# Channel attention and two feed-forward layers in one kernel: operands of the second pair prepared beside the last plain units, Silu ahead of a split, the last q and k tiles loaded singly

## The chip, the core and the metric

The kernel runs on one core of a Trainium2 chip. The metric is device time in microseconds of one execution; the median of three runs is given. Engines are named as in the profile: PE or TensorE (matmul), PEld (its weight loads), DVE (VectorE), ACT (ScalarE), POOL (GpSimd), SP (SyncE, which issues the DMAs).

## What is computed

Three steps over N = 6016 tokens and C = 256 channels, in float32:

```python
qn = q / (norm(q, axis=1) + 1e-6); kn = k / (norm(k, axis=1) + 1e-6)   # norms over the tokens
a  = softmax(kn.T @ qn / tau)                                          # 256 x 256
x  = v @ a                                                             # 6016 x 256
x  = (silu(x @ w_gate) * (x @ w_val)) @ w_out                          # layer 1: 256 -> 1536 -> 256
h  = x @ w_in;  x = (h * clip(h + 3, 0, 6) / 6) @ w_out2               # layer 2: 256 -> 2048 -> 256
```

The weights reach the core as 64-bit floats.

## The kernel before

**Accuracy.** Each matmul of the feed-forward layers is made of three (mm3, L91): every operand is split into a high part (ACT copies it to a rounded type) and a low part (DVE subtracts the high part from the original), and high x high, low x high and high x low are summed. So every operand of a matmul costs one ACT and one DVE instruction, each of 128x512 as a rule.

**Weights.** Each tile of 64-bit weights is a Job (L103): load, cut (two DVE instructions: exponent and mantissa bits), power (two ACT activations), mantissa and sign (DVE), scale (DVE product), and for w_out a split into `wo`. pump (L271) moves three jobs one step each; the jobs of layer 1 run during the plain units. convert (L252) moves the jobs of layer 2, whose scalings, sums and subtractions are on POOL, and stores the result in memory (wi_d, w2_d).

**Attention.** q and k are read in chunks of 1, 1, 2, then fourteen of 3, then one of 1 tile of 128 tokens, five chunks ahead (L410 to L420); ACT squares them, DVE adds the squares up in acc, TensorE accumulates k.T q. norms (L487) sums acc over the tokens and makes the two scalings; softmax follows. TensorE transposes the result into `early`. keep_warm (L434) issues matmuls whose result is not used.

**Folding.** v @ a is never formed: a is multiplied into w_gate and w_val instead. fold(m, g) (L606) multiplies one weight tile on TensorE, ACT scales the result out of the bank into FA, then ACT and DVE split it into the layer's weights w1. The closures that it returns (`lows`) are the DVE splits; those of the first two folds are called once by hand and again in unit 1, since the list is not emptied between.

**Plain units.** The tokens are six pairs of two blocks (512 tokens each, the last pair 448). Pair 0 is computed plainly: 24 units (L904), one for each of 12 tiles of the hidden layer and each of two blocks: twelve matmuls into two banks, ACT takes Silu of one, DVE multiplies by the other, the product h is split into hl, and three units later back() (L824) multiplies it by `wo` (six matmuls, tile `o`). ps_f has four banks (a, d, b0, b1), taken in turn.

**Cubes.** The other pairs go through seven products instead of eight (class Cube, L673; p1 to p7, three matmuls each) for a 2x2 arrangement of two hidden tiles and two blocks. Their seven operands, sums and differences of the four quarters of x, are made by prep(u) (L327): nine steps s1 to s9, each a split or a difference, put in the list `todo`; work(n) (L396) runs n steps of that list. Each split operand lies in a staging tile (stage, L320: two tiles `st`, or operand tiles that are free), is stored to memory, and is loaded again when its pair begins (arrive, L951; load_op, L400). In a cube ACT copies p1's bank (a) into bank b, applies Silu to bank a after p2 (after_p2, L774) and to x12 after p3 (after_p3, L780). The split of cube i's r11 stands in late3 (L812), which the loop (L962) calls in cube i+1 ahead of that cube's p2. layer 2's cubes have a clipped product in place of Silu.

**What sets the order.** The program is scheduled by hand (L407): each engine runs its instructions in the order in which the code issues them, and waits on semaphores for the other engines. prep(1) is appended to `todo` behind the last weight sums, by a step that issues its load (prep_steps, L388); it starts in unit 22, and the rest is run by arrive(1, ...) behind the last unit.

Of the kernel before, what the change touches and what calls it, by code (L numbers as in the profile page):

```python
# [18 lines left out]
def channel_attention_then_two_ffns(  # L19
# [24 lines left out]
    nc = tc.nc  # L44
# [273 lines left out]
    places_st = [0]  # L318

    def stage(u):  # L320

        i = places_st[0] = places_st[0] + 1
        if 0 < u < NP or u >= NP and i % 4 < 2:
            return op_p.tile([P, 2, TB], F32R, tag=f"op{(NQ * (u + 1) + i % 2) % NS}", name="sp")
        return st_p.tile([P, 2, TB], F32R, tag="st", name="st")

    def prep(u):  # L327

        n = pairs[u % NP][1]
        x = load_v(u) if u < NP else load_x2(u - NP)  # L330
        b11, b21, b12, b22 = x[:, 0, 0, :n], x[:, 0, 1, :n], x[:, 1, 0, :n], x[:, 1, 1, :n]
        opd[u] = dram.tile([P, NQ, 2, TB], F32, tag=f"opd{u}", name="opd")
        of = {0: b11, 1: b11, 2: b22, 3: b21, 4: b22, 5: b12, 6: b21}
        t = {}

        def hi(j):
            t[j] = stage(u - 1)
            nc.scalar.activation(t[j][:, 0, :n], of[j], AF.Copy)

        def lo(j):  # L340
            nc.vector.tensor_tensor(  # L341
                out=t[j][:, 1, :n], in0=of[j], in1=t[j][:, 0, :n].bitcast(F32), op=ALU.subtract
            )
            stored.add((u, j))
            nc.sync.dma_start(out=opd[u][:, j, :, :n], in_=t[j][:, :, :n].bitcast(F32))

        def diff(out, a, b):
            nc.vector.tensor_tensor(out=out, in0=a, in1=b, op=ALU.subtract)  # L348

        def s1():  # L350
            hi(0)

        def s2():
            hi(4)
            lo(0)
# [32 lines left out]
    def prep_steps(u):  # L388
        def load():
            todo[2:2] = prep(u)  # L390

        return [load, lambda: None, lambda: None]

# [13 lines left out]
    with tc.manual_schedule():  # L407

        with tc.tile_pool(name="sm", bufs=1) as sm, tc.tile_pool(name="qk", bufs=AHEAD) as qk_p, tc.tile_pool(
# [5 lines left out]
            while sum(sizes) < NT:  # L415
                sizes.append((NT - sum(sizes) + 1) // 2)
# [13 lines left out]
            WARM = (1, 11, 2)  # L430
# [56 lines left out]
            def norms():  # L487
# [11 lines left out]
                v_hi(0)  # L499
# [3 lines left out]
                )  # L503
                nc.scalar.activation(nrm, ss_ps, AF.Sqrt, bias=tiny)
# [23 lines left out]
            for i, (n0, n) in enumerate(chunks):  # L528
# [10 lines left out]
                if i == len(chunks) - 2:  # L539
                    nc.vector.tensor_tensor(out=acc[:, 1], in0=acc[:, 1], in1=acc[:, 2], op=ALU.add)  # L540
                if i == len(chunks) - 1:
                    nc.vector.tensor_tensor(out=acc[:, 0], in0=acc[:, 0], in1=acc[:, 1], op=ALU.add)
# [18 lines left out]
            pump(steps=(1,))  # L561
# [16 lines left out]
            pump(steps=(2,))  # L578
# [9 lines left out]

            keep_warm(WARM[2])
# [16 lines left out]
        def fold(m, g):  # L606
# [15 lines left out]
            fa = FA[g % 2]  # L622
            for c in range(CT):
                nc.scalar.activation(fa[:, (c, 3 - c)[m]], ps[:, c, :], AF.Copy, scale=rden[:, c : c + 1])
            o = CT * m
# [47 lines left out]
        class Cube:  # L673
# [106 lines left out]
            def after_p3(self):  # L780
                self.add(self.x12, self.x12, self.d)
                if self.layer == 1:
                    self.silu(self.x12)
                else:
                    hl = self.hi(self.r11)
                    self.lo(hl, self.r11, 0, 0)
                    self.r12 = self.relu(self.x12)
# [24 lines left out]
            def late3(self):  # L812
                x = self.r11 if self.layer == 1 else self.r21
                self.lo(self.hi(x), x, 0, 1)
# [62 lines left out]
        pump(steps=(2,))  # L877
        nc.scalar.activation(warm, three, AF.Silu)
        need(0, 0)
        need(1, 0)  # L880
        lows = [fold(0, 0)]
        v_hi(1)
        lows.append(fold(1, 0))
        pump(steps=(3, 2))
        for go in lows:
            go()
        v_lo(1)
        pump(steps=(1,))
        todo.append(w1_sums(0))

# [13 lines left out]
        for i, (f, b) in enumerate(units):  # L904
# [27 lines left out]
            work(2 if i > 18 else 1)  # L932
            g = i // 4 + 1
            if i % 4 in (1, 2) and g < NG1:
# [13 lines left out]
        plain_split(lambda: pump())  # L948
        todo[:0] = w1_rest(NG1 - 1)

        def arrive(u, n, *js):  # L951
            for j in js:
                while (u, j) not in stored:
                    work(1)
                load_op(u, j, n)

        arrive(1, pairs[1][1], 0, 1)
        arrive(1, pairs[1][1], 2, 3, 4, 5, 6)
# [3 lines left out]
        for c, key in enumerate(cubes):  # L962
# [15 lines left out]
            if layer == 1 and c % 4 == 1 and not converted():  # L978
                convert()
# [21 lines left out]
            cube.after_p3()  # L1001
# [52 lines left out]
```

## Time and profile before

| | |
|---|---|
| median of three runs | 1142.75 us (1142.6 to 1143.39) |
| the profiled execution | 1143.76 us, span 1142.0 us |
| TensorE busy | 1106.2 us (97%), 4900 matmuls |
| DVE, ACT, POOL busy | 807.2 (71%), 760.2 (67%), 81.4 us (7%) |
| mean granted TensorE clock | 0.989 |
| DMA | 157.65 MB, mean 138 GB/s |

The span runs from the first to the last instruction of the program; the profiled execution's own time has 1.76 us more. A matmul's end is modelled, so "busy" of TensorE says little about its pace; what it waits for, and the clock that it was granted, say more. Roughly: attention to 57 us, the plain units of pair 0 to 178 us, layer 1's cubes to 640 us, layer 2's cubes to the end.

### The profile page before, as it was taken

The page shows a single profiled execution, that of the slowest core. Times are in us where ns is not written, and L with a number is a line of the kernel's source. Part 1 is how long each engine was busy: PE and PEld are TensorE (multiplying, and loading weights), DVE is VectorE, ACT ScalarE, POOL GpSimd, SP SyncE. Part 2 cuts the span into 40 slices and gives each one's busy share as a digit, 9 for nine tenths or more (in the row PEclk, how much of TensorE's full clock was granted, in tenths as well). Part 3 has the DMA queues.
Part 4 walks back from the last instruction along what each step waited for, and adds up shares of the span by engine and source line. Part 5 has one row for each costly group of instructions (what it writes and reads, how often), then busy time and mean ns, then how long its engine had stood idle before and what let it go on. Part 6 is the DMA issues. An engine that isn't in the chain of part 4 may idle for free.

```text
span 1142.0 us, 13730 instructions
## 1 busy us (share of the span) xinstructions
PE 1106.2 (97%) x4900; PEld 918.4 (80%) x4900; DVE 807.2 (71%) x1252; ACT 760.2 (67%) x1323; POOL 81.4 (7%) x92
## 2 busy tenths in 40 slices
PE   8989995999999999999999999999999999999998
PEld 6768883877877877788899888888888888888897
DVE  6989953577787777766566568667677677676665
ACT  6767643566766766675566577677767777776766
POOL 0000000122322222320000000000000000000000
PEclk9999997999999999999999999999999999999999
DMA  8622305433733634532355752422523413414100
GB/s 327 253 74 93 129 1 195 173 132 118 247 135 130 230 143 148 200 134 84 115 187 203 273 192 93 148 111 82 177 88 113 168 56 130 142 65 131 68 1 32
DMA packets 58340, 157.65 MB, mean 138 GB/s; under 512 B 5280, under 2 KB 17312, under 8 KB 56864
## 3 DMA queue, kind: packets, MB, share of 16 engines
q1 hardware_dynamic: 58272, 156.78, 38.4%
q8 instruction: 38, 0.62, 0.2%
q14 instruction: 30, 0.25, 0.1%
HBM read 93.45 MB, written 63.31 MB: 137 GB/s over the span
## 4 chain that ended last, share of the span: by engine, by line
PE 67%; DVE 14%; ACT 7%; DMA 3%; issue 3%; DVEq 0%; SPq 0%; ACTq 0%
PE o L96 31%; PE ps_b L96 15%; PE ps_d L96 10%; PE ps_a L96 10%; ACT hl L702 3%; DVE h L759 3%; DVE hl L768 2%; DVE h L706 2%; DMA op<-opd 1%; DVE sp L341 1%; ACT e L127 1%; ACT e L126 1%; DMA vr<-in_vT 1%; DVE vr L348 1%; ACT h L702 1%
## 5 line engine op out<-in xcount | busy, mean ns | idle before, releaser
L768 DVE TENSOR_TENSOR hl<-h,hl 128x512 fp32r<-128x512 f32 (+1 forms) x312 | 211.9, 692 | 210.2 <-ACT hl L702 205.0
L96 PE MATMUL o<-hl,w2o 128*128 128x512 f32 (+1 forms) x1152 | 287.6, 385 | 0.0
L702 ACT ACTIVATE hl<-h 128x512 fp32r<-128x512 f32 (+1 forms) x312 | 188.0, 618 | 100.0 <-DVE h L752 53.5
L96 PEld LDWEIGHTS o<-hl,w2o 128*128 128x128 f32 x1152 | 216.0, 188 | 40.8 <-DVE hl L768 0.7
L96 PE MATMUL o<-hl,wo 128*128 128x512 f32 (+1 forms) x864 | 220.3, 391 | 0.0
L96 PEld LDWEIGHTS o<-hl,wo 128*128 128x128 f32 x864 | 164.0, 190 | 31.4
L96 PE MATMUL ps_b<-op,w 128*128 128x512 f32 (+1 forms) x540 | 142.0, 388 | 3.1 <-DMA op<-opd 3.1
L96 PEld LDWEIGHTS ps_b<-op,w 128*128 128x128 f32 x540 | 101.1, 188 | 24.9 <-issue 3.8
L96 PE MATMUL ps_a<-op,w 128*128 128x512 f32 (+1 forms) x360 | 102.2, 392 | 14.4 <-DMA op<-opd 9.9
L96 PE MATMUL ps_b<-op,w2i 128*128 128x512 f32 (+1 forms) x432 | 112.0, 385 | 0.0
L96 PE MATMUL ps_d<-op,w 128*128 128x512 f32 (+1 forms) x360 | 102.9, 394 | 2.6 <-DVE h L706 1.7
L96 PEld LDWEIGHTS ps_b<-op,w2i 128*128 128x128 f32 x432 | 81.1, 188 | 15.1
L702 ACT ACTIVATE h<-ps_b 128x512 f32<-128x512 f32 (+1 forms) x108 | 63.3, 586 | 43.5 <-PE ps_b L96 41.9
L96 PEld LDWEIGHTS ps_a<-op,w 128*128 128x128 f32 x360 | 67.0, 190 | 31.1 <-ACT h L741 8.3
L746 ACT ACTIVATE h<-h,three 128x512 f32<-128x512 f32 (+1 forms) x96 | 68.7, 716 | 33.3 <-DVE h L706 31.7
L706 DVE TENSOR_TENSOR h<-h,ps_b 128x512 f32<-128x512 f32 (+1 forms) x108 | 72.4, 671 | 15.6 <-PE ps_b L96 15.3
L96 PEld LDWEIGHTS ps_d<-op,w 128*128 128x128 f32 x360 | 66.9, 190 | 19.9 <-DVE h L706 6.6
L96 PE MATMUL ps_d<-op,w2i 128*128 128x512 f32 (+1 forms) x288 | 79.8, 385 | 0.3 <-DMA op<-opd 0.3
L96 PE MATMUL ps_a<-op,w2i 128*128 128x512 f32 (+1 forms) x288 | 79.8, 385 | 0.0
L706 DVE TENSOR_TENSOR h<-h,ps_d 128x512 f32<-128x512 f32 (+1 forms) x108 | 72.2, 669 | 10.3 <-PE ps_d L96 10.3
L702 ACT ACTIVATE ps_b<-ps_a 128x512 f32<-128x512 f32 (+1 forms) x108 | 61.9, 573 | 25.9 <-PE ps_a L96 25.7
L752 DVE SCALAR_TENSOR_TENSOR h<-h 128x512 f32<-128x512 f32 (+1 forms) x96 | 65.1, 678 | 12.6 <-ACT h L746 12.6
(128 smaller groups left out, 1321.2 us busy)
## 6 DMA issues: line engine op xcount, KB each, us to landing
op<-opd SPq DMA_DIRECT2D x63, 512.0 KB, 5.0
opd<-sp SPq DMA_DIRECT2D x42, 512.0 KB, 2.7
opd<-st SPq DMA_DIRECT2D x21, 512.0 KB, 2.6
raw<-in_moe_w_out SPq DMA_DIRECT2D x14, 512.0 KB, 4.2
w2i<-wi_d SPq DMA_DIRECT2D x4, 1792.0 KB, 8.2
op<-opd SPq DMA_DIRECT2D x14, 448.0 KB, 4.2
tq<-in_q SPq DMA_DIRECT2D x14, 384.0 KB, 6.7
tk<-in_k SPq DMA_DIRECT2D x14, 384.0 KB, 7.2
```

Of the source, the lines that this page charges most:

```text
L96: nc.tensor.matmul(out, lhsT=w, rhs=x, start=first, stop=last, skip_group_check=True)
L126: nc.scalar.activation(e.bitcast(F32), e, AF.Relu, scale=-4.0, bias=exp_top)
L127: nc.scalar.activation(e, e.bitcast(F32), AF.Relu, scale=-1.0, bias=exp_span)
L341: nc.vector.tensor_tensor(out=t[j][:, 1, :n], in0=of[j], in1=t[j][:, 0, :n].bitcast(F32), op=ALU.subtract)
L348: nc.vector.tensor_tensor(out=out, in0=a, in1=b, op=ALU.subtract)
L702: nc.scalar.activation(out[:, : self.n], src[:, : self.n], AF.Copy)
L706: nc.vector.tensor_tensor(out=out[:, :n], in0=a[:, :n], in1=b[:, :n], op=ALU.add)
L746: nc.scalar.activation(r[:, : self.n], x[:, : self.n], AF.Relu, bias=three)
L752: nc.vector.scalar_tensor_tensor(out=r[:, :n], in0=r[:, :n], scalar=6.0, in1=x[:, :n], op0=ALU.min, op1=ALU.mult)
L759: nc.vector.tensor_tensor(out=h[:, :n], in0=h[:, :n], in1=x[:, :n], op=ALU.mult)
L768: nc.vector.tensor_tensor(out=hl[:, 1, :n], in0=h[:, :n], in1=hl[:, 0, :n].bitcast(F32), op=ALU.subtract)
```

## The change

1. prep(u, direct): operands named in `direct` are split straight into their operand tile, with no store and no load. For pair 1 these are operands 0, 1 and 4. Their steps (steps1) are made in unit 10, where the load of v is issued, and appended to `todo` where prep_steps stood; work(3) instead of work(2) runs from unit 19, with the last weight sums put ahead of it; units 22 and 23 issue the loads of operands 2, 5 and 3, 6. One staging place more (op6).
2. convert() begins in the units behind 18, once the jobs of layer 1 are done, and is called once in a cube; the second call in every fourth cube is gone.
3. In layer 1's cubes the high part of r11 is copied in after_p3 of the next cube (behind Silu of bank a) and subtracted behind DVE's add into x12.
4. The last chunk of three q and k tiles is read as three of one tile, so there are four single chunks at the end; the two sums over acc stand two chunks earlier.
5. Around softmax: the split of v's first block and the fields of the fourth job (w_val, g = 1) stand elsewhere, its power and scale later; two warming matmuls are gone; Silu's table is loaded behind the first folds.
6. The first two folds split their weights straight from the bank (ACT writes the high part, DVE subtracts it), and FA is written after; their splits are made once.

```diff
-    places_st = [0]
+    places_st = [-1]
     def stage(u):
         i = places_st[0] = places_st[0] + 1
+        if u == 0 and i % 3 == 0:
+            return op_p.tile([P, 2, TB], F32R, tag="op6", name="sp")
...
-    def prep(u):
+    def prep(u, direct=()):
...
         def hi(j):
-            t[j] = stage(u - 1)
+            t[j] = op_tile(u, j) if j in direct else stage(u - 1)
...
+            if j in direct:
+                return
             stored.add((u, j))
...
-            while sum(sizes) < NT:
-                sizes.append((NT - sum(sizes) + 1) // 2)
+            sizes = sizes[:-1] + [1] * (NT - sum(sizes[:-1]))
...
-            WARM = (1, 11, 2)
+            WARM = (1, 11)
...
-                v_hi(0)
                 jobs[passed[1]].cut()
...
+                jobs[passed[1]].mantissa()
                 nc.scalar.activation(nrm, ss_ps, AF.Sqrt, bias=tiny)
...
-            pump(steps=(1,))
+            v_hi(0)
...
-            pump(steps=(2,))
+            jobs[passed[1]].sign()
             v_lo(0)
...
+            if g == 0:
+                his, los = ([w_in[1, 0][:, :, part, o + (c, 1 - c)[m], :] for c in range(CT)] for part in range(2))
+                srcs = [ps[:, c, :].rearrange("p (c f) -> p c f", c=2) for c in range(CT)]
+                for c in range(CT):
+                    nc.scalar.activation(his[c], srcs[c], AF.Copy, scale=rden[:, c : c + 1])
+                    nc.vector.scalar_tensor_tensor(
...
-            def after_p3(self):
+            def after_p3(self, prev):
+                if prev and prev.layer == 1:
+                    hl = prev.hi(prev.r11)
+                    if self.layer == 2:
+                        prev.lo(hl, prev.r11, 0, 1)
                 self.add(self.x12, self.x12, self.d)
                 if self.layer == 1:
+                    if prev:
+                        prev.lo(hl, prev.r11, 0, 1)
                     self.silu(self.x12)
...
             def late3(self):
-                x = self.r11 if self.layer == 1 else self.r21
-                self.lo(self.hi(x), x, 0, 1)
+                if self.layer == 2:
+                    self.lo(self.hi(self.r21), self.r21, 0, 1)
...
-        pump(steps=(2,))
-        nc.scalar.activation(warm, three, AF.Silu)
+        v_hi(1)
         need(0, 0)
         need(1, 0)
-        lows = [fold(0, 0)]
-        v_hi(1)
-        lows.append(fold(1, 0))
-        pump(steps=(3, 2))
-        for go in lows:
-            go()
+        fold(0, 0)
+        fold(1, 0)
         v_lo(1)
-        pump(steps=(1,))
+        nc.scalar.activation(warm, three, AF.Silu)
+        jobs[passed[1]].power()
+        passed[1] += 1
+        load_jobs()
+        lows = []
...
-            work(2 if i > 18 else 1)
+            if i % 4 == 0 and i:
+                todo[:0] = w1_rest(i // 4 - 1)
+            work(3 if i > 18 else 1)
+            if i > 18 and passed[3] == NJ1:
+                convert()
+            if i == 10:
+                steps1 = prep(1, (0, 1, 4))
...
-                        todo.extend(prep_steps(1))
-            if i % 4 == 0 and i:
-                todo[:0] = w1_rest(i // 4 - 1)
+                        todo.extend(steps1)
+            if i >= len(units) - 2:
+                for j in ((2, 5), (3, 6))[i - len(units) + 2]:
+                    arrive(1, pairs[1][1], j)
...
-        arrive(1, pairs[1][1], 0, 1)
-        arrive(1, pairs[1][1], 2, 3, 4, 5, 6)
...
-            if layer == 1 and c % 4 == 1 and not converted():
-                convert()
...
-            cube.after_p3()
+            cube.after_p3(prev)
```

How the change moves instructions, at three places. First SP's queue from the last units on, before (opd: staged operands in memory; op: operand tiles; vr: v's rows; wi_d, raw: weights of layer 2):

```order
L307 DMA vr<-in_vT 128x2x512 x2
L345 DMA opd<-st 128x1024 x3
L402 DMA op<-opd 128x1024 x2
L345 DMA opd<-st 128x1024 x2
L402 DMA op<-opd 128x1024
L345 DMA opd<-st 128x1024
L402 DMA op<-opd 128x1024 x3
L345 DMA opd<-st 128x1024
L402 DMA op<-opd 128x1024
```

and now:

```order
L307 DMA vr<-in_vT 128x2x512 x2
L109 DMA raw<-in_moe_w_out 128x2x512 x2
L109 DMA raw<-in_moe_w_in 128x2x512
L109 DMA raw<-in_moe_w_out 128x2x512
L349 DMA opd<-sp 128x1024
L349 DMA opd<-st 128x1024
L109 DMA raw<-in_moe_w_in 128x2x512
L349 DMA opd<-st 128x1024
L349 DMA opd<-sp 128x1024
L400 DMA op<-opd 128x1024 x4
L213 DMA wi_d<-st 128x2x384
```

Seven stores and seven loads in turn have become four stores and then four loads, and the load of v stands ahead of four weight loads.

Second, DVE from the last sum over acc to softmax, before (raw, e, m: the job of w_val; dg: the scaling of one side; nmx: the row maximum):

```order
L542 TENSOR_TENSOR acc<-acc 128x512
L117 TENSOR_SCALAR e<-raw 128x512
L120 TENSOR_SCALAR m<-raw 128x512
L501 TENSOR_SCALAR half<-half,tau_sb 128x2
L505 RECIPROCAL rno<-nrm 128x4
...
L511 TENSOR_SCALAR dg<-ident,rno 128x128 x2
L131 SCALAR_TENSOR_TENSOR m<-raw,m 128x512
L137 SCALAR_TENSOR_TENSOR m<-raw,m 128x512
L566 SCALAR_TENSOR_TENSOR s_sb<-s_sb,rno,bc 128x256
```

and now:

```order
L117 TENSOR_SCALAR e<-raw 128x512
L120 TENSOR_SCALAR m<-raw 128x512
L497 TENSOR_SCALAR half<-half,tau_sb 128x2
L131 SCALAR_TENSOR_TENSOR m<-raw,m 128x512
L502 RECIPROCAL rno<-nrm 128x4
...
L508 TENSOR_SCALAR dg<-ident,rno 128x128 x2
L563 SCALAR_TENSOR_TENSOR s_sb<-s_sb,rno,bc 128x256
L571 TENSOR_REDUCE nmx<-s_sb 128x1
...
L137 SCALAR_TENSOR_TENSOR m<-raw,m 128x512
```

The mantissa (L131) has moved ahead of the norms, the sign (L137) behind softmax's maxima; the two cuts (L117, L120) still stand ahead of the norms.

Third, ACT in one cube of layer 1, before (hl_3378: high part of x12 of the cube before; sp: a staged operand; h_3399: copy of p6; hl_3401: high part of r11 of the cube before):

```order
L702 ACTIVATE hl_3378<-h_3330 128x512
L338 ACTIVATE sp_3381<-vr_3190 128x512
L702 ACTIVATE h_3399<-ps_b_3370 128x512
L702 ACTIVATE hl_3401<-h_3338 128x512
L741 ACTIVATE h_3407<-ps_a_3366 128x512
L741 ACTIVATE h_3399<-h_3399 128x512
```

and in a cube now:

```order
L712 ACTIVATE hl_3369<-h_3326 128x512
L340 ACTIVATE sp_3372<-vr_3186 128x512
L712 ACTIVATE h_3390<-ps_b_3361 128x512
L751 ACTIVATE h_3395<-ps_a_3357 128x512
L712 ACTIVATE hl_3400<-h_3331 128x512
L751 ACTIVATE h_3390<-h_3390 128x512
```

Silu of bank a (L741, now L751) and the high part of r11 have changed places.

## Rows read from the trace of the kernel before

**Rows 1.** What TensorE waited for, whole span: total us, times, longest us
```profile
PE ps_a L96 <- DMA op<-opd: 9.9, 2, 6.5
PE ps_a L96 <- ACT h L741: 4.3, 5, 1.3
...
PE ps_d L96 <- DVE w L637: 3.2, 2, 3.0
...
PE ps_d L96 <- DVE h L706: 1.7, 2, 0.8
```

**Rows 2.** Busy windows: us, sum, PE PEld DVE ACT POOL (x), PEclk, DMA, GB/s
```profile
178.50:206.00 27.50, 13.53 (x32) 8.93 (x32) 8.55 (x14) 7.79 (x13) 0.00 (x0) 0.63 0.72 231
206.00:233.00 27.00, 27.00 (x121) 22.33 (x120) 18.39 (x28) 19.38 (x37) 5.45 (x7) 1.00 0.36 134
```

**Rows 3.** ACT's waits from 172 to 200 us; the page's DMA issues (us to landing)
```profile
ACT st L338 <- DMA opd<-st: 9.3, 3, 5.0
...
op<-opd SPq DMA_DIRECT2D x63, 512.0 KB, 5.0
...
opd<-st SPq DMA_DIRECT2D x21, 512.0 KB, 2.6
```

**Rows 4.** Timeline of a cube of layer 1: start, us, what, [idle before <-releaser]
```profile
238.17 1.29 POOL L191 TENSOR_TENSOR st<-e,st 128x512 fp32r<-128x512 f32 x1 [7.18 <-ACT st L215]
238.21 1.80 DVE L759 TENSOR_TENSOR h<-h 128x512 f32<-128x512 f32 x1
...
244.22 0.63 ACT L702 ACTIVATE hl<-h 128x512 fp32r<-128x512 f32 x1 [2.54 <-DVE h L759]
...
245.39 0.97 PE L96 MATMUL ps_a<-op,w 128*128 128x512 f32 x3 [1.29 <-ACT h L741]
```

**Rows 5.** DVE's timeline at the end of attention
```profile
48.25 0.42 DVE L117 TENSOR_SCALAR e<-raw 128x512 uint32<-128x512 uint32 x1
...
49.77 0.18 DVE L505 RECIPROCAL rno<-nrm 128x4 f32<-128x4 f32 x1 [0.63 <-ACT nrm L504]
...
52.68 0.47 DVE L566 SCALAR_TENSOR_TENSOR s_sb<-s_sb,rno,bc 128x256 f32<-128x256 f32 x1
```

**Rows 6.** SP's issues at the end of attention
```profile
34.32 0.33 SPq L423 DMA_DIRECT2D tq<-in_q  x1
...
36.91 0.33 SPq L423 DMA_DIRECT2D tq<-in_q  x1
...
39.28 0.41 SPq L109 DMA_DIRECT2D raw<-in_moe_w_val  x1
```

**Rows 7.** DMA issues from 213 to 215 us and from 38 to 40.5 us: KB, us to landing
```profile
vr<-in_vT SPq DMA_DIRECT2D x2, 512.0 KB, 4.2
raw<-in_moe_w_in SPq DMA_DIRECT2D x1, 512.0 KB, 5.5
...
raw<-in_moe_w_val SPq DMA_DIRECT2D x1, 512.0 KB, 7.4
```

**Rows 8.** Timelines from the fold to the first o, and a busy window
```profile
56.18 1.28 ACT L878 ACT_TABLE_LOAD   x1
56.76 3.62 PE L614 MATMUL ps_b<-early 128*128 128x256 f32 x16
58.69 0.84 ACT L624 ACTIVATE FA<-ps_b,rden 128x256 f32<-128x256 f32 x2 [1.01 <-PE ps_b L614]
...
64.97 0.72 ACT L126 ACTIVATE e<-e,exp_top 128x512 f32<-128x512 uint32 x1 [2.30 <-DVE e L117]
...
66.97 0.69 DVE L930 TENSOR_TENSOR h<-h,ps_d 128x512 f32<-128x512 f32 x1 [0.24 <-ACT h L929]
...
81.02 1.52 PE L96 MATMUL o<-hl,wo 128*128 128x512 f32 x6
...
73.00:76.00 3.00, 3.00 (x9) 2.29 (x9) 2.96 (x7) 2.16 (x4) 0.00 (x0) 0.56 0.49 169
```

**Rows 9.** DVE's timeline in unit 19
```profile
161.06 0.69 DVE L930 TENSOR_TENSOR h<-h,ps_d 128x512 f32<-128x512 f32 x1 [1.33 <-PE ps_d L96]
```

More of the change, by code (lines that the diff above doesn't have):

```diff
@@ L386, in prep @@
         return [s1, s2, s3, s4, s5, s6, s7, s8, s9]
[L388 to L392, printed above, removed]
     todo = []
@@ L538, in channel_attention_then_two_ffns @@
                 nc.vector.tensor_tensor(out=acc[:, :n], in0=acc[:, :n], in1=sq[:, :n], op=ALU.add)
-                if i == len(chunks) - 2:
+                if i == len(chunks) - 4:
                     nc.vector.tensor_tensor(out=acc[:, 1], in0=acc[:, 1], in1=acc[:, 2], op=ALU.add)
-                if i == len(chunks) - 1:
+                if i == len(chunks) - 3:
                     nc.vector.tensor_tensor(out=acc[:, 0], in0=acc[:, 0], in1=acc[:, 1], op=ALU.add)
@@ L587, in channel_attention_then_two_ffns @@
             nc.vector.reciprocal(out=rden, in_=den)
-            keep_warm(WARM[2])
         w1_p = ctx.enter_context(tc.tile_pool(name="w1", bufs=1))
@@ L622, in fold @@
             fa = FA[g % 2]
+            o = CT * m
+            if g == 0:
[4 more added lines that the diff above has]
+                    nc.vector.scalar_tensor_tensor(
+                        out=los[c],
+                        in0=srcs[c],
+                        scalar=rden[:, c : c + 1],
+                        in1=his[c].bitcast(F32),
+                        op0=ALU.mult,
+                        op1=ALU.subtract,
+                    )
             for c in range(CT):
                 nc.scalar.activation(fa[:, (c, 3 - c)[m]], ps[:, c, :], AF.Copy, scale=rden[:, c : c + 1])
-            o = CT * m
+            if g == 0:
+                return lambda: None
             w1_hi(g, o, fa[:, o : o + 2])
@@ L874, in next_weights, with arrive @@
                 nc.sync.dma_start(out=t[:, :nf].bitcast(F32), in_=w2_d[:, f0 : f0 + nf])
-        pump(steps=(2,))
-        nc.scalar.activation(warm, three, AF.Silu)
+        v_hi(1)
         need(0, 0)
         need(1, 0)
-        lows = [fold(0, 0)]
-        v_hi(1)
-        lows.append(fold(1, 0))
-        pump(steps=(3, 2))
-        for go in lows:
-            go()
-        v_lo(1)
-        pump(steps=(1,))
-        todo.append(w1_sums(0))
+        fold(0, 0)
+        fold(1, 0)
+        v_lo(1)
+        nc.scalar.activation(warm, three, AF.Silu)
[3 more added lines that the diff above has]
+        lows = []
+        todo.append(w1_sums(0))
+        def arrive(u, n, *js):
+            for j in js:
+                while (u, j) not in stored:
+                    work(1)
+                load_op(u, j, n)
         units = [(f, b) for f in range(NF1) for b in range(2)]
@@ L942, in channel_attention_then_two_ffns @@
                     if g == NG1 - 1:
-                        todo.extend(prep_steps(1))
-            if i % 4 == 0 and i:
-                todo[:0] = w1_rest(i // 4 - 1)
+                        todo.extend(steps1)
+            if i >= len(units) - 2:
+                for j in ((2, 5), (3, 6))[i - len(units) + 2]:
+                    arrive(1, pairs[1][1], j)
             while len(backs) > LAG - 1:
                 back()
-        plain_split(lambda: pump())
+        plain_split(lambda: None)
         todo[:0] = w1_rest(NG1 - 1)
[L951 to L955, printed above, removed]
-        arrive(1, pairs[1][1], 0, 1)
-        arrive(1, pairs[1][1], 2, 3, 4, 5, 6)
         prev = None
```

## The prediction, made before the change was run

> **What bounds the kernel now.** I read the waits of TensorE first. Over the whole span it waits for few things [rows 1]: 9.9 us for operand tiles of ps_a that come back from memory, 4.3 us for ACT's Silu (L741), 3.2 us for a weight split (L637), 1.7 us for DVE's copies out of ps_d. Everything else is matmul work that the change leaves alone: TensorE's instructions are the same, in the same order, but for two warming matmuls. So what can be won is time in which TensorE stands or runs at half clock, and I looked for each such place.
>
> The largest is the change from pair 0 to pair 1. Between 178.5 and 206.0 TensorE issues 32 matmuls, at a mean granted clock of 0.63; in the 27 us behind, it issues 121 at 1.00, 0.223 us each [rows 2]. 32 matmuls are worth 7.1 us, so this stretch loses 27.5 - 7.1 = **20.4 us**. The cause is a chain: the plain units' last `o` group ends at 178.5, prep(1) begins only two units before that, ACT stands 9.3 us for staging buffers that are still being stored, a store lands after 2.6 us and a load after 5.0 [rows 3].
>
> The second place is the cubes of layer 1 in pairs 1 to 5. ACT's copy of r11 (L702) waits 2.54 us for a DVE product at 244.22, the Silu that frees bank a stands behind it in ACT's queue, and p1 of the next cube starts 1.29 us late [rows 4]. DVE is late there because convert() has put two cuts ahead of the product, and because GpSimd is busy: a product that takes about 0.7 us took 1.80 while a GpSimd subtract of 1.29 us ran [rows 4].
>
> The third is the end of attention, where DVE's chain of norms and softmax sets when the first weights are folded.
>
> **Part A: operands of pair 1 prepared beside the last units.** Removed: three stores and three loads (operands 0, 1, 4 are split straight into their operand tiles). Moved: all seven splits and four differences, from behind the units into units 19 to 23, and with them the first conversions of layer 2's weights. Four operands (2, 5, 3, 6) still go to memory and back.
>
> Is there room on DVE? The product of unit 19 begins at 161.06 [rows 9]. From its end at 161.7 to the product of unit 23 DVE now has 29 instructions: four sums (1.5 us), seven splits and four differences (6.7), two cuts of 0.34 twice (1.4), a mantissa and a sign (1.2), a weight split (1.1), four hl splits and three products (4.3): 16.2 us, so 177.9 at the earliest. ACT's copies stand between them and make DVE wait some 2 us more, and GpSimd starts its part at about 174.7; I add 1 us for it. I take 180.5 for that product's start, between 177.9 (nothing waits) and 183 (each of five GpSimd instructions holds DVE up by 1.1 us, the excess in [rows 4]). TensorE reaches p5 at 179.2 and needs this product, so it stands 2 us; p5 and an `o` group (nine matmuls, 2.0 us) bring it to 183.2. The last staged split ends about 2 us before the product, its store is issued at 179, the four loads are behind it in SP's queue: the first lands at 179.2 + 5.0 = 184.2, the third, which p2 needs, 2 x 1.3 us later at 186.8 (1.3 us is the step from the vr pair, median 4.2, to the third transfer, 5.5 [rows 7]). From p2 on 15 matmuls remain to the end of p7: 186.8 + 3.3 = 190.1. Without any wait the 30 matmuls from 178.5 would end at 185.2. So 5 us stay exposed, plus about 1 us for a chance of one half-clock stretch. **A = -20.4 + 6 = -14.4 us**; ends: -18 (DVE at 177.9, loads in 4.2 us), -10 (183, and the clock down).
>
> **Part B: Silu of bank a ahead of the copy of r11, DVE's add ahead of r11's split, no second convert() in every fourth cube.** Both stalls lose their cause: 4.3 + 1.7 = 6.0 us [rows 1]. The copy now comes behind the Silu; its `o` group is issued after p7, p1 and p5 of the next steps, over 3 us later. I keep 0.5 us for new clashes: **B = -5.5**; ends -7 and -1. The remaining convert() calls reach further into pair 4, which no load waits for.
>
> **Part C: end of attention and first fold.** The q and k tiles now end in four singles, two more requests, each waiting for a chunk of five before; the requests of this queue step by 2.59 us (34.32 to 36.91), so the last q request moves from 36.91 to 42.1, and w_val's raw tile, issued 2.37 us after it, from 39.28 to 44.46 [rows 6]. A raw tile behind the two vr transfers landed after 5.5 us on an empty queue, after 7.4 on a full one [rows 7]; here the queue is empty, so it lands at 50.0 (upper end 51.9). But DVE's cut of this tile stood at 48.25 [rows 5] and still stands ahead of the norms: it waits. Behind it come the second cut, the scaling of half and the mantissa, now moved ahead of the reciprocal: 0.34 + 0.34 + 0.2 + 0.7. The reciprocal starts at 51.5 instead of 49.77 [rows 5], and all norms queue behind. The mantissa and sign that stood between the norms and the scaling of s_sb (52.68) are gone from there, worth about 0.6. So softmax is 1.1 us late; dropping two warming matmuls gives back 0.5, and the fold starts at 57.3 instead of 56.76 [rows 8].
>
> The first fold's weights are split straight from the bank, ACT copying and DVE subtracting in turn. 1.93 us after the fold's start [rows 8] come four copies of 0.42, four DVE pieces of 0.47 and four FA copies of 0.42, one after the other: 5.3 us, to 64.6. Then the table load (1.28, before it stood ahead of the fold and was hidden), two exponent activations (1.4) and Silu (0.6): the first product starts at 68.1 instead of 66.97 [rows 8]. The program makes them wait for each other; if the two engines overlapped, it would be some 1.5 us less. The Trainium skill (PSUM — Partial Sum Buffer, "PSUM bank collisions raise a hardware error") says that any two engines on one bank must be kept apart, reads included: by it the turns stay, and the sum is as I have it; no run here shows the case without them.
>
> What it saves: the two splits that the old code made twice (L637, up to 3.0 us of stall [rows 1]) vanish. What it costs: the job behind w_val is scaled one unit later, and so wo of the first back product. From 68.1 DVE has, up to that split, three products, four sums, three scalings, three sets of fields (2.1 each), two hl and one weight split: 13.9 us, so it ends at 82.0, where TensorE's first `o` (81.02 [rows 8]) needs it for its second matmul. TensorE is then 0.8 us later than now; it stands 3 us before that, and after such a gap it now ran 3 us at a clock of 0.56, 9 matmuls where 13 go in at full clock [rows 8]: 1 us, with an even chance. **C = +0.8 + 0.5 = +1.3**; ends -1 (the raw tile in time) and +4 (landing at 51.9, clock down).
>
> **Sum.** -14.4 - 5.5 + 1.3 = -18.6. The profiled execution took 1143.76 us (span 1142.0), 1.0 above the median of the runs, 1142.75: 1125.2 against its own time, **1124.2** against the median.
>
> **Rivals.**
> 1. The raw tile is in time, or DVE hides it: C = -1, 1122. For it: only one row puts its landing at 5.5. Against: it must come 1.5 us sooner. Chance 0.15.
> 2. GpSimd holds DVE up. For it: 1.80 us against 0.7 [rows 4], and the change moves eight GpSimd instructions into 174 to 181. Each of five DVE instructions then loses 1.1 us, A is 4.5 us less, 1129. The Trainium skill (SBUF — State Buffer, "SBUF: two separate sides") has the rule: a DVE instruction with two SBUF inputs and a GpSimd one that reads SBUF exclude each other for the whole instruction; the trace agrees. Against: other pairs there overlap. Chance 0.15.
> 3. The later split of r11 delays its `o` group: B = 0, 1130. Against: 3 us of slack. Chance 0.1.
> 4. The change does not shorten the way through memory as it should: the four staged operands are stored so late that TensorE waits as long for p6 as now for p7; A = -6, 1133. Chance 0.08.
> 5. **Slower**: staging holds ACT. ACT's queue holds the staged copies between the units' Silus. If each waits for a store, as now (9.3 us [rows 3]), the Silus behind wait too, TensorE stands 9.3 us inside the units, and two round trips (2 x 7.6) stay behind them: 24.5 us against 20.4 now, with C +1.3 and B 0: 1148. It decides if more than one staged copy waits; there are three places (two st, one op6) for four copies, so only the last should. Chance 0.03.
>
> **Numbers.** My forecast, 1124.2, has 0.45; 0.04 is left for better than 1117 (A and B at their good ends, C at -1). The range 1117 to 1131 holds the forecast with its bounds and rivals 1 to 3, and leaves out 4, 5 and the ends. A measurement of this kernel can tell 0.2%, 2.3 us, from no change. Faster 0.95, same 0.02, slower 0.03: only several rivals together give no change.
>
> **What would show it.** In the new profile: TensorE's wait of ps_a for op<-opd falls from 9.9 us to 2 to 4; waits for the Silu of ps_a are gone; DVE waits for the raw tile at about 48.5; a wait of `o` for wo at 79 to 82. The forecast is wrong if ACT waits for staging stores inside units 20 to 23, or if the products of those units are over 3 us late.

## The result and the profile after

The change takes **1124.73 us** (median of four runs, 1123.83 to 1128.53) against 1142.67 before: ratio 0.9848, 95% interval 0.9825 to 0.9871. The prediction was 1124.2. The profiled execution is the longest of the four, 1128.53 us (span 1126.7). A second trace of the same kernel (`change_again`, below) took 1124.45, so numbers of the change are given from both where they differ.

The time falls into four stages, cut at four places of TensorE's timeline: the start of the units' last `o` group, the first p7, the first matmul of layer 2, the last `o` group. For the kernel before these starts are 177.12, 205.19, 651.73 and 1134.18. For the change TensorE's timeline has:

```profile
182.27 1.52 PE L96 MATMUL o<-hl,wo 128*128 128x512 f32 x6
...
190.26 0.94 PE L96 MATMUL ps_b<-op,w 128*128 128x512 f32 x3 [0.81 <-DMA op<-opd]
192.72 1.65 PE L96 MATMUL ps_a<-op,w 128*128 128x512 f32 x3 [1.52 <-DMA op<-opd]
...
196.95 0.84 PE L96 MATMUL ps_b<-op,w 128*128 128x512 f32 x3
...
635.17 0.86 PE L96 MATMUL ps_a<-op,w2i 128*128 128x512 f32 x3
...
1118.85 3.95 PE L96 MATMUL o<-hl,w2o 128*128 128x448 f32 x18
```

The differences of such starts, in us, for all kernels that ran (the first column is the start itself; the names are those of the next section):

| kernel | last o of the units | to p7 | layer 1 | layer 2 | median, us |
|---|---|---|---|---|---|
| before | 177.12 | 28.08 | 446.5 | 482.5 | 1142.7 |
| the change | 182.27 | 14.68 | 438.2 | 483.7 | 1124.73 |
| `change_again` | 180.94 | 13.23 | 437.1 | 483.7 | 1124.22 |
| `cut_late` | 177.24 | 12.91 | 436.3 | 483.5 | 1119.58 |
| `fold_fa` | 179.73 | 15.36 | 435.9 | 483.9 | 1123.68 |
| `a_undone` | 182.27 | 26.95 | 434.1 | 483.5 | 1135.97 |
| `load_order` | 182.42 | 12.02 | 436.1 | 483.8 | 1123.88 |
| `r11_before` | 181.59 | 13.33 | 451.3 | 482.4 | 1136.59 |
| `s1_late` | 181.74 | 13.21 | 433.1 | 483.6 | 1121.35 |
| `phase_less` | 181.38 | 15.49 | 433.6 | 483.5 | 1123.66 |
| `fourth` | 181.59 | 13.97 | 435.1 | 483.6 | 1123.66 |
| `b2` | 177.06 | 9.22 | 433.1 | 482.3 | 1111.83 |
| `b2_chunks` | 176.12 | 9.30 | 433.1 | 482.3 | 1111.35 |
| `b2_fa` | 174.25 | 9.72 | 433.1 | 482.3 | **1108.29** |

So the profiled execution of the change loses 5.2 us up to the last units, wins 13.4 in the way into pair 1, wins 8.3 in layer 1 and loses 1.2 in layer 2: -15.3 together. What TensorE waits for now, whole span, against [rows 1]:

```profile
PE ps_b L96 <- ACT h L712: 3.9, 4, 1.3
PE bc L556 <- DVE dg L508: 1.7, 1, 1.7
...
PE o L96 <- DVE wo L159: 1.6, 1, 1.6
PE ps_a L96 <- DMA op<-opd: 1.5, 1, 1.5
PE ps_d L96 <- DVE h L952: 1.4, 1, 1.4
```

The waits for Silu of bank a (L741, 4.3 us) and for DVE's L706 (1.7) are gone, that of ps_a for operands fell from 9.9 to 1.5. New are four waits, 3.9 us, of p7 for ACT's copy out of bank b, and single waits in and behind the units: for a product (L952, 1.4) and for wo's split (1.6). bc's wait in the norms grew from 0.7 to 1.7.

### The profile page after: what moved, and what is told of

Read it like the earlier page. It is cut to its first block, busy times and chain, and to the rows that moved or that the text cites. A ratio compares the mean times of both kernels' runs of the same rounds, so it can differ in the third digit from the quotient of the medians.

```text
span 1126.7 us, 13789 instructions
## 1 busy us (share of the span) xinstructions
PE 1100.6 (98%) x4896; PEld 922.0 (82%) x4896; DVE 797.7 (71%) x1254; ACT 765.5 (68%) x1329; POOL 81.4 (7%) x92
## 4 chain that ended last, share of the span: by engine, by line
PE 85%; DMA 7%; DVE 4%; ACT 2%; issue 1%; SPq 0%; DVEq 0%; ACTq 0%
PE o L96 37%; PE ps_b L96 20%; PE ps_a L96 13%; PE ps_d L96 13%; DMA x_d<-xo 2%; DMA vr<-in_vT 1%; DMA op<-opd 1%; DVE acc L535 1%; DMA tk<-in_k 1%; PE ps_b L609 1%; DMA tq<-in_q 1%; DMA raw<-in_moe_w_val 1%; DVE m L131 0%; PE warm L435 0%; DVE h L952 0%
## 5 line engine op out<-in xcount | busy, mean ns | idle before, releaser
L96 PE MATMUL ps_d<-op,w 128*128 128x512 f32 (+1 forms) x360 | 100.1, 387 | 1.4 <-DVE h L952 1.4
L716 DVE TENSOR_TENSOR h<-h,ps_b 128x512 f32<-128x512 f32 (+1 forms) x108 | 72.4, 671 | 13.1 <-PE ps_b L96 11.8
```

Of the source, the lines that this page charges most:

```text
L96: nc.tensor.matmul(out, lhsT=w, rhs=x, start=first, stop=last, skip_group_check=True)
L716: nc.vector.tensor_tensor(out=out[:, :n], in0=a[:, :n], in1=b[:, :n], op=ALU.add)
```

## The experiments

**The change a second time.** No edit.

> The changed kernel once more, unaltered, as the measure for the other runs and for a second trace. Its profiled execution took 1128.53 us, the three others 1123.83 to 1125.18. One theory: the 3 to 4 us lie in the clock ahead of the fold (0.50 from 50 to 58 in the trace), so a run without that shows a first product near 67 to 68 instead of 71.2 and takes 1124. The rival: the half clock there belongs to the change and comes in each run; then the first product stays at 71 and the 4 us are found elsewhere.

1124.22 us (1123.57 to 1126.15). The half clock ahead of the fold is there again, as the windows (columns as in [rows 2]) show for the change and for this run; the granted clock is 0.57 in both, and was 1.00 before:

```profile
48.00:60.00 12.00, 9.92 (x45) 8.99 (x45) 6.53 (x21) 5.02 (x12) 0.00 (x0) 0.57 0.37 127
```

```profile
48.00:60.00 12.00, 9.88 (x44) 8.97 (x44) 6.88 (x21) 4.71 (x11) 0.00 (x0) 0.57 0.38 130
```

The rival holds: it belongs to the change. The 4 us between the two executions lie elsewhere: between the first product and the last `o` (111.07 against 109.43, with a granted clock of 0.79 against 1.00 from 84 to 92), on the way to p7 (1.45) and in layer 1 (1.1).

**Cuts behind the norms.**

```diff
-                jobs[passed[1]].cut()
...
-                jobs[passed[1]].mantissa()
                 nc.scalar.activation(nrm, ss_ps, AF.Sqrt, bias=tiny)
...
                         out=dg[:, d, :], in0=ident, scalar1=rno[:, d : d + 1], scalar2=None, op0=ALU.mult
                     )
+                jobs[passed[1]].cut()
...
+            jobs[passed[1]].mantissa()
             jobs[passed[1]].sign()
```

> The two cuts of the raw tile of w_val behind the norms instead of ahead of them, its mantissa behind softmax's maxima. Theory: DVE's wait for the tile (2.43 us at 50.49) holds the norms; without it the reciprocal starts at 49.6 instead of 51.9, TensorE does not stand long enough to lose its clock, the fold starts at 56.5 to 57.5 instead of 59.97, and the time is 3 to 5 us shorter than the change's (1120 to 1122). Rival: the fold is set by the warming matmuls and the softmax chain on ACT, or the late cut only moves the wait to the scale of w_val; then the fold starts later than 59 or the first product stays near 71, and the time is within 1 us of the change's.

1119.58 us, 4.6 below `change_again`, as the theory had it. DVE in the change, then in this run:

```profile
46.57 1.49 DVE L535 TENSOR_TENSOR acc<-acc,sq 128x512 f32<-128x512 f32 x2
50.49 0.43 DVE L117 TENSOR_SCALAR e<-raw 128x512 uint32<-128x512 uint32 x1 [2.43 <-DMA raw<-in_moe_w_val]
...
51.90 0.17 DVE L502 RECIPROCAL rno<-nrm 128x4 f32<-128x4 f32 x1
```

```profile
47.49 1.49 DVE L534 TENSOR_TENSOR acc<-acc,sq 128x512 f32<-128x512 f32 x2
48.89 0.22 DVE L496 TENSOR_SCALAR half<-half,tau_sb 128x2 f32<-128x2 f32 x1
50.41 0.18 DVE L500 RECIPROCAL rno<-nrm 128x4 f32<-128x4 f32 x1 [1.30 <-ACT nrm L499]
```

From the end of the sums to the reciprocal it is 3.84 us with the wait and 1.43 without. (The edit also takes the two cuts and the mantissa out of this stretch; DVE stands 1.30 us there for ACT's root instead.) The wait costs more than itself: behind it 22 warming matmuls, which softmax's transposes must let pass, took 4.90 us in the change, 2.99 here and 2.62 before (TensorE's timelines: the change, this run, before):

```profile
54.33 4.90 PE L435 MATMUL warm<-ones 128*128 128x128 f32 x22
```

```profile
52.85 2.99 PE L435 MATMUL warm<-ones 128*128 128x128 f32 x22
...
56.53 3.72 PE L609 MATMUL ps_b<-early 128*128 128x256 f32 x16 [0.20 <-ACT early L582]
```

```profile
51.84 2.62 PE L438 MATMUL warm<-ones 128*128 128x128 f32 x22
```

The fold starts at 56.53 here, 59.97 in the change.

**Folds split from FA.**

```diff
-            if g == 0:
+            if False:
...
-            if g == 0:
-                return lambda: None
...
-        fold(0, 0)
-        fold(1, 0)
+        lows = [fold(0, 0), fold(1, 0)]
+        for go in lows:
+            go()
```

> Part 6 undone alone: the first two folds are scaled into FA first, and the high and low parts are made from FA, once each. Theory: the turns of ACT and DVE on the bank (5.7 us from 62.13 to 67.8 in the trace of the change) hold ACT's table load, exponent and first Silu; from FA ACT needs 2.8 us for both folds and waits for no DVE, the first product comes 2 to 3 us earlier (68 to 69 where the change has 71.2), and the time is 2 to 3 us shorter than the change's 1124.2. Rival: the first product is set by the table load and the exponent behind it, and wo's split by DVE's chain; then the time stays within 1 us.

The place behaves as the theory has it, the time does not: the first product starts 8.67 us behind the fold instead of 11.23, yet the median is 1123.68 (1119.1 to 1124.8). In its trace the units' last `o` is 1.2 us earlier than in `change_again` and the way to p7 2.1 longer, with one more wait for the loads. ACT in the change takes turns with DVE on the bank:

```profile
62.13 0.47 ACT L623 ACTIVATE w<-ps_b,rden 128x256 fp32r<-128x256 f32 x1 [0.90 <-ACT v L475]
63.15 0.47 ACT L623 ACTIVATE w<-ps_b,rden 128x256 fp32r<-128x256 f32 x1 [0.55 <-DVE w L624]
...
67.82 1.28 ACT L900 ACT_TABLE_LOAD   x1
```

From FA ACT is done with both folds at 65.3 and loads the table then. Where the gain went can be read from the clock. From the first product to the units' last `o` it is 111.05 us here and 109.43 in `change_again`: here TensorE runs at a granted clock of 0.83 from 84 to 92, behind the wait for wo's split, there at 1.00. Of the traces of all kernels above but `before`, only `change_again` and `cut_late` (109.47) were spared this; the others have 110.9 to 111.1. On the way to p7 the third load landed 11.25 us behind the last `o` instead of 10.31, and TensorE ran at 0.57 from 192 to 196. Of the four runs, the one of 1119.1 us has a mean granted clock of 0.997, the others 0.992 to 0.994. So the gain was lost in the clock for the most part; why the loads landed later stays open.

**Part 1 undone.** prep(1) without `direct`, behind the units; with it the conversions begin in the cubes instead of the units, with the second one in every fourth cube again.

```diff
-            work(3 if i > 18 else 1)
-            if i > 18 and passed[3] == NJ1:
-                convert()
-            if i == 10:
-                steps1 = prep(1, (0, 1, 4))
+            work(2 if i > 18 else 1)
...
-                        todo.extend(steps1)
+                        todo.extend(prep_steps(1))
...
+        arrive(1, pairs[1][1], 0, 1)
+        arrive(1, pairs[1][1], 2, 3, 4, 5, 6)
...
+            if layer == 1 and c % 4 == 1 and not converted():
+                convert()
```

> Part 1 undone: all seven operands of pair 1 stored and loaded again, prepared behind the last units as before; the conversions begin in the cubes, with the second one in every fourth cube as before (without that they would not be done in time). Theory: the stretch from the last o of the units to the end of the first p7 loses 19 to 21 us again where the change loses about 7; time 1136 to 1139, 12 to 15 above the change's 1124.2. Rival: the loss in this stretch comes mostly from the clock, or from the load of v, and not from the stores and loads; then the time is under 1133.

1135.97 us. The way from the last `o` to p7 is 26.95 us again, 13.7 more than in `change_again`, with the waits for operands back (9.8 us at ps_a, as in [rows 1], and 2.9 at ps_b). Its layer 1 is 3.0 us shorter and the units' last `o` 1.3 later, so the time is 11.8 longer and not 13.7. The start of the conversions moved along with part 1 here, so the 3.0 us are not those of part 1 alone.

**Operands in the order of use.**

```diff
-                for j in ((2, 5), (3, 6))[i - len(units) + 2]:
+                for j in ((2, 3), (5, 6))[i - len(units) + 2]:
```

> The four staged operands of pair 1 loaded in the order 2, 3, 5, 6 instead of 2, 5, 3, 6. p2 needs operand 3 right behind p6's operand 2. Theory: p2's wait of 0.9 to 1.5 us falls by the step between two loads (1.3 us), p7 then waits less than that, and the stretch at half clock behind it may go too; time 1 to 2.5 us shorter. Rival: TensorE then waits as long at p7 or p4, or for ACT and DVE of unit 23; time within 0.7 us.

p2's wait is gone and the way to p7 is 1.2 us shorter (12.02), but the median, 1123.88, can't be told from 1124.22. The time is the rival's, its cause is not: no wait came up elsewhere on the way. The loads land as before; with the wait gone the `o` group ahead of p6 (2.77 us) and part of p6 still run at half clock (0.58 from 188 to 192), and the half clock behind the wait for wo's split, which `change_again` was spared, is there (111.04 us from the first product to the last `o`).

**Part 3 undone.**

```diff
             def after_p3(self, prev):
-                if prev and prev.layer == 1:
-                    hl = prev.hi(prev.r11)
...
-                    if prev:
-                        prev.lo(hl, prev.r11, 0, 1)
...
             def late3(self):
-                if self.layer == 2:
-                    self.lo(self.hi(self.r21), self.r21, 0, 1)
+                x = self.r11 if self.layer == 1 else self.r21
+                self.lo(self.hi(x), x, 0, 1)
```

> Part 3 undone alone: the high part of r11 again ahead of p2 of the next cube, ahead of Silu. Theory: the later split of r11 makes the last o group of a pair late, with it the store of the result, the buffer of v's rows and the load of v; undone, the load of v is issued 3 to 4 us earlier within its pair and the p7 waits (3.9 us) vanish. Silu of bank a is late again where DVE is late, but without the second conversion in every fourth cube: 1 to 4 us of waits of ps_a come back, time 1122 to 1128. Rival: the 8.2 us gained in layer 1 came from the order of ACT's queue wholly, and the second conversion mattered nothing; then over 6 us come back and the time is over 1128.

1136.59 us, 12.4 above `change_again`; layer 1 takes 451.3 us against 437.1. The rival holds: part 3 (ACT's order, and with it DVE's add ahead of r11's split) is worth 14.2 us, more than all of layer 1's gain of 9.4. And p7's waits did not go, so my theory of their cause falls:

```profile
PE ps_b L96 <- ACT h L712: 3.6, 4, 1.9
PE ps_a L96 <- ACT h L751: 3.0, 8, 0.5
```

**First step of the next pair behind p7.**

```diff
-            work(1)
+            if (layer, i) != (1, 2):
+                work(1)
...
             cube.after_p7()
+            if (layer, i) == (1, 2):
+                work(1)
```

> In the third cube of a pair of layer 1 the first step of preparing the next pair (ACT's copy of a part of v) stands behind p7 instead of ahead of p4. Theory: the new waits of p7 for ACT's copy of p6 (3.9 us in four waits) come from this copy, which waits for v's rows; they vanish, and the time is 4 to 5 us shorter than the change's (1120). Rival: bank b's copy is late by itself or the wait goes to the end of the pair, where the last operands are then stored later; then TensorE's sum of waits in layer 1 stays within 1 us of 3.9.

1121.35 us, 2.9 below `change_again` where 4 to 5 were expected; no wait of TensorE is left in layer 1, which takes 433.1 us, 4.0 less. The rest was lost ahead of it, again in the half clock behind the wait for wo's split (111.05 us from the first product to the last `o`). The wait of p7 was ACT's copy of v in front of the copy of p6. Why v is late the next run shows.

**Conversions one unit later.**

```diff
-            if i > 18 and passed[3] == NJ1:
+            if i > 18 + 1 and passed[3] == NJ1:
```

> The conversions begin one unit later (behind unit 19 instead of 18), so that each falls one cube later in its pair. Theory: v's rows come late because the stores of the pair's result stand in SP's queue behind a conversion's two stores and a weight load, and the buffer of v's rows comes free only when they have landed; shifted by one, the result's stores stand ahead of these (as the order of the queue shows), they land 2 to 4 us earlier within the pair, the four waits of p7 for ACT (2.7 us, 3.2 to 4 with the clock) fall under 1 us, and the time is 2 to 4 us shorter: 1120 to 1122. Rival: v's rows are late because r11's later split makes the last o group late; then the waits stay and the time is within 1 us.

Layer 1 takes 433.6 us, 3.5 less: the theory holds. SP's queue at the change from one pair to the next, in the change and then here:

```profile
380.54 0.37 SPq L217 DMA_DIRECT2D wi_d<-st  x1
381.00 0.42 SPq L109 DMA_DIRECT2D raw<-in_moe_w_out  x1
381.52 2.92 SPq L869 DMA_DIRECT2D x_d<-xo  x4
389.73 0.90 SPq L307 DMA_DIRECT2D vr<-in_vT  x2
```

```profile
379.52 3.30 SPq L869 DMA_DIRECT2D x_d<-xo  x4
384.83 0.90 SPq L307 DMA_DIRECT2D vr<-in_vT  x2
385.82 0.41 SPq L213 DMA_DIRECT2D wi_d<-st  x1
```

v's rows and the result share one buffer, so v's load (L307) waits for the result's stores to land. In the change these stand behind a conversion's store and a weight load, and the last landed 6.1 us after its issue; here each landed 2.0 to 2.3 us after its issue. With one conversion in each of a pair's twelve cubes every pair meets the conversions in the same phase. But the whole time, 1123.66, is that of the change: the way to p7 became 2.3 us longer. Product and Silu of unit 23 came earlier, TensorE then waited for the loads instead and ran at half clock:

```profile
189.12 0.93 PE L96 MATMUL ps_b<-op,w 128*128 128x512 f32 x3 [2.12 <-DMA op<-opd]
191.58 1.65 PE L96 MATMUL ps_a<-op,w 128*128 128x512 f32 x3 [1.52 <-DMA op<-opd]
```

**The second conversion again.**

```diff
+            if layer == 1 and c % 4 == 1 and not converted():
+                convert()
             if len(backs) > 2 - layer:
```

> The second conversion in every fourth cube of layer 1 again, all else as in the change. If layer 1's gain (8.2 us where 5.5 were forecast) came in part from dropping it, TensorE's waits in layer 1 grow by 2 us or more and the time is 1126 to 1128. If ACT's order alone gave it, the time stays within 1.5 us of 1124.2; the wait for v's rows, once in each pair at the same step of the conversions, would then come in some pairs only, since the conversions no longer keep step with the pairs.

1123.66 us, the same within the measurement; layer 1 is 435.1, 2.0 less, with one wait of p7 (0.4 us) instead of three. Dropping the call won nothing; it put the conversions in step with the pairs.

**The repairs together.** `b2` has the edits of `cut_late` and `load_order`, 18 + 2 for the conversions, and

```diff
+        nc.scalar.activation(warm, three, AF.Silu)
         v_hi(1)
...
         v_lo(1)
-        nc.scalar.activation(warm, three, AF.Silu)
...
-                if prev and prev.layer == 1:
+                if prev and self.layer == 1:
                     hl = prev.hi(prev.r11)
-                    if self.layer == 2:
-                        prev.lo(hl, prev.r11, 0, 1)
...
-            def late3(self):
+            def late3(self, layer=2):
+                if layer == 2 and self.layer == 1:
+                    self.lo(self.hi(self.r11), self.r11, 0, 1)
...
-                prev.late3()
+                prev.late3(layer)
```

`b2_chunks` has the last q and k tiles as before as well, and `b2_fa` also the edit of `fold_fa`:

```diff
-            sizes = sizes[:-1] + [1] * (NT - sum(sizes[:-1]))
+            while sum(sizes) < NT:
+                sizes.append((NT - sum(sizes) + 1) // 2)
...
-                if i == len(chunks) - 4:
+                if i == len(chunks) - 2:
...
-                if i == len(chunks) - 3:
+                if i == len(chunks) - 1:
```

> The repairs together: cuts behind the norms, Silu's table ahead of the folds, operands loaded in the order 2, 3, 5, 6, conversions two units later (each two cubes later in its pair, so the result's stores and the load of v stand ahead of a conversion's stores), and in the first cube of layer 2 r11's split ahead of p2 as before. Theory: they touch different waits and add up: 4.6 for the cuts, 2.7 to 4 for p7's waits, 0.3 to 1 for the loads, 1.3 for the table, 0.8 to 1.3 for layer 2's first cube: 1112 to 1115. Rival: a wait that one of them frees is taken by the next engine (DVE at wo's split, the four loads behind the last store), then 1116 to 1119.

> As the repairs together, with the last q and k tiles read as a chunk of three and one single as before. Theory: the four singles brought nothing by themselves (the last sum over acc ends at 48.06 in the change, 48.33 before, with the first matmuls 0.68 us earlier), so this lies within 1 us of the run with singles. Rival: singles let TensorE and DVE finish sooner and are hidden by the late cut; then this one is over 1 us longer.

> The repairs with q and k's last tiles as a chunk and one single, and the first two folds split from FA. Theory: the first product comes 2 to 2.5 us earlier behind the fold (with the split from FA alone it came at 68.7 instead of 71.2), nothing behind it takes that back, since the way into pair 1 hardly waits any more; 1109 to 1110. Rival: the time won before the units is lost again in the clock behind the wait for wo's split, as in that run; then it lies within 1 us of 1111.35.

1111.83, 1111.35 and 1108.29 us (ratio 0.9693, interval 0.9677 to 0.9709). The repairs add up, to a little more than expected. The four singles brought nothing (1111.37 to 1112.09 with them, 1110.85 to 1111.63 without). Here the split from FA wins 3.1 us by the medians (1.6 between the two profiled executions), and layer 2's loss went too (482.3). What each of the other repairs gives in this company was not measured. The first of TensorE's waits over the whole span in the last of them, and its window to set beside the two above:

```profile
PE s L516 <- DMA tk<-in_k: 4.5, 4, 3.5
PE o L96 <- DVE wo L159: 1.7, 1, 1.7
```

```profile
48.00:60.00 12.00, 10.21 (x61) 8.44 (x61) 7.38 (x22) 9.57 (x21) 0.00 (x0) 1.00 0.17 46
```

## Why the prediction was right, and where by luck

**Part A (-14.4) held**: -13.4 and -14.9 in the two traces, 13.7 when undone. Counted from the units' last `o`, the steps came within 0.8 us of where they were put: the product of unit 23 4.1 us behind it (forecast 3.4, 180.5), the first load issued at 2.8 and landed at 7.9 (forecast 2.1 and 7.1). Rival 2 was there in small. DVE, then GpSimd, in units 22 and 23:

```profile
180.90 1.19 DVE L343 TENSOR_TENSOR st<-vr,st 128x512 fp32r<-128x512 f32 x1
182.12 0.83 DVE L352 TENSOR_TENSOR vr<-vr 128x512 f32<-128x512 f32 x1
183.70 0.95 DVE L343 TENSOR_TENSOR sp<-vr,sp 128x512 fp32r<-128x512 f32 x1 [0.75 <-ACT sp L340]
...
185.25 1.22 DVE L923 TENSOR_TENSOR hl<-h,hl 128x512 fp32r<-128x512 f32 x1
```

```profile
179.94 1.60 POOL L150 TENSOR_TENSOR m<-m,e 128x512 f32<-128x512 f32 x1 [177.14 <-DVE m L137]
181.62 0.79 POOL L179 TENSOR_TENSOR e<-m 128x128 f32<-128x128 f32 x1
...
183.65 0.45 POOL L182 TENSOR_TENSOR e<-m,e 128x128 f32<-128x128 f32 x1
```

Each of the first three DVE instructions, 0.69 us alone, ends 0.54 to 0.55 us behind the GpSimd instruction that ran when it began (182.09 behind 181.54, 182.95 behind 182.41, 184.65 behind 184.10), as if it began only then. The Trainium skill (SBUF — State Buffer, "SBUF: two separate sides") says that a DVE instruction with two SBUF inputs and a GpSimd one that reads SBUF exclude each other for the whole instruction. The trace agrees; the product at 180.30, one of whose inputs is a bank, took its 0.68 us beside the first of these GpSimd instructions. All four together lost 1.4 us, not the 4.5 of the rival, which put 1.1 us on each of five: the three shown lost 0.50, 0.14 and 0.26, since GpSimd's instruction was over by more than half when they began, or took only 0.45 us.

**Part C (+1.3) was mis-sized**: +5.2, and 3.8 in the second trace. Of the 5.2, 3.2 lie ahead of the fold, 1.0 between fold and product, 0.9 behind it. The order of events was right, step by step: the raw tile landed at 50.47 (forecast 50.0), the reciprocal started at 51.9 (51.5), wo's split ended 13.9 us behind the first product (13.9). The step that failed is "dropping two warming matmuls gives back 0.5, and the fold starts at 57.3": it started at 59.97, since the 22 remaining ones ran at half clock. I had an even chance of half clock at the first `o` (it came in one trace of the two, for 1.6 us), and none here, where the wait I forecast myself leaves TensorE idle for 1.7 us. The turns on the bank stayed, as the sum had it, and cost 2.6 us between fold and product (`fold_fa`).

**Part B (-5.5) was mis-sized the other way**: -8.3 and -9.4. Two errors are in it. First, "Both stalls lose their cause: 4.3 + 1.7 = 6.0 us" took the listed idle time for the loss. TensorE before, in the cube of [rows 4]:

```profile
243.25 0.84 PE L96 MATMUL ps_b<-op,w 128*128 128x512 f32 x3
245.39 0.97 PE L96 MATMUL ps_a<-op,w 128*128 128x512 f32 x3 [1.29 <-ACT h L741]
...
250.07 0.85 PE L96 MATMUL ps_a<-op,w 128*128 128x512 f32 x3
```

and the same groups in the change:

```profile
235.21 0.84 PE L96 MATMUL ps_b<-op,w 128*128 128x512 f32 x3
...
239.97 0.84 PE L96 MATMUL ps_a<-op,w 128*128 128x512 f32 x3
```

From p7 at 243.25 to the p2 at 250.07 it is 6.82 us; the same groups in the change take 4.76. The loss is 2.06 us where 1.29 are listed: the groups behind a late start come later too. Over all of layer 1 the table gives the same: 446.5 us before against 433.1 where no wait is left (`s1_late`), so 13.4 us were lost where the list has 6.0. What ACT waited for there (from 207 us to the end of layer 1) shows it better, before and after:

```profile
ACT h L741 <- DVE h L706: 50.7, 57, 1.8
ACT hl L702 <- DVE h L759: 44.5, 55, 2.6
...
ACT sp L338 <- DMA vr<-in_vT: 3.6, 4, 1.5
```

```profile
ACT h L712 <- PE ps_b L96: 48.4, 45, 1.9
ACT ps_b L712 <- PE ps_a L96: 37.9, 39, 1.3
ACT hl L712 <- DVE h L769: 18.5, 20, 1.4
ACT sp L340 <- DMA vr<-in_vT: 16.2, 4, 4.5
```

ACT waited for DVE, so TensorE for ACT; now ACT waits mostly for TensorE. Second, the new clash was put at 0.5 us and is 4.0 (`s1_late`): "The remaining convert() calls reach further into pair 4, which no load waits for" looked at the loads of weights and not at the load of v behind the conversions' stores in SP's queue.

**Layer 2 (+1.2) was not in the sum**: the split of the last r11 of layer 1 now stands right ahead of the `o` group that needs it, which waits 0.6 us for ACT.

The four errors (+1.0, -2.8, +3.9, +1.2) leave 3.3 us in the profiled execution; against the median, where the change's profiled run is 3.8 above, they nearly cancel. That the median came 0.5 us from the forecast is luck: B gave 2.8 to 3.9 us more than its sum, C 2.5 to 3.9 less. Of the signs, ps_a's wait for operands fell further than said (1.5 us against 2 to 4), the waits for Silu went, DVE waited for the raw tile from 48.1, and `o` waited for wo at 83.1 to 85.2, later than the 79 to 82 said since the fold was late. The rivals 3 to 5 did not come; rival 1 had the wrong direction.

## What to carry to other kernels

An instruction that is moved ahead in one queue also moves what it waits for: look up, for each wait in front of a chain, whether its data is now requested later. Work that recurs with the period of the loop (one conversion in each cube) meets the loop's own transfers at the same place each time; shift it by one step and look at the queue's order. The idle time listed for a wait is not its loss: in layer 1 the loss was over twice the listed time (13.4 against 6.0 us), on the way to p7 a listed wait went and the median stayed (`load_order`). Compare the starts of the same groups with and without it, and the granted clock behind it, before one trace is set against another.

## What the runs showed that was not expected

Two executions of one kernel differed by 4 us, 1.6 of them because TensorE ran at half clock (0.79 of its full 2.4 GHz on average from 84 to 92 us) behind the same 1.6 us wait in one and not in the other. Matmuls meant to keep the clock up became the delay themselves once it was down (22 of them, 4.90 us against 2.62). And three repairs that shortened their own stage (`phase_less`, `load_order`, `fold_fa`) left the total where it was, since the way to p7 or the clock took the gain back; together they counted: `b2_fa`, which has all three (the conversions shifted by one unit more) and two repairs that were not run alone (Silu's table ahead of the folds, r11's split in layer 2's first cube), is 15.9 us below `change_again`, where `cut_late` and `s1_late`, the only two that gained alone, make 7.5.
